# Second layer's output product by one level of Strassen's algorithm instead of a plain product

## The chip, the cores and the metric

The kernel runs on one NeuronCore of one Trainium2 chip. The metric is device time in microseconds (us): of the kernel before, three runs took 610.71, 610.83 and 611.26, median 610.83. Engines are named as in the profile: PE is TensorE (PEld its weight loads), DVE is VectorE, ACT is ScalarE, POOL is GpSimd, SP is SyncE, which issues most DMAs.

## What is computed

A retention layer feeds two dense layers. Its state decays by head, and everything is float32:

```python
for t in range(S):                                   # B, H, S, D = 2, 8, 768, 64
    state = gamma * state + einsum('bhd,bhe->bhde', k[:, :, t], v[:, :, t])
    y[:, :, t] = scale * einsum('bhd,bhde->bhe', q[:, :, t], state)
x = y.transpose(0, 2, 1, 3).reshape(B * S, H * D)    # 1536 x 512
y = ((x @ w_a) * (x @ w_b)) @ w_out                  # 512 -> 1536 -> 512
h = y @ w_in                                         # 512 -> 2048
g = np.maximum(0.01 * h, h)
out = g @ w_out2                                     # 2048 -> 512
```

The inputs of `w_*` reach the device as 64-bit words that are rounded to float32 there.

## The kernel before

Tokens are cut into three tiles of 512 (`t` = 0, 1, 2), features into blocks of 128. A float32 operand is split into a high half, rounded to the matmul's input format (a cast on ACT), and a low half (a subtraction on DVE); `split` (L81) does that, and `mm3` (L88) forms a product from three matmuls: high x high, low x high and high x low. Each matmul loads 128 x 128 weights and streams up to 512 columns into one PSUM bank. PSUM has eight banks.

Four stages follow each other on PE: retention (loop L406), the products with w_a and w_b (`ab_step`), the product with w_out of the first layer (loop L460), and the second layer (loop L505), about 344 us into the span. The order of all instructions is the order of the program text; there is no planner. Weights are loaded by SP into four `raw` buffers, rounded by six operations (`begin_weights`, `round_steps`, on ACT and DVE) and split when `want` asks. `ahead(rate)` rounds weights early, as long as the pool of 80 tiles of 128 x 512 (`slots`) has room. `tnew` gives one of ten further tiles.

In the second layer, for each tile of tokens `t` and each of 16 blocks `f` of inner features, `h2_step` makes one block of h (12 matmuls), ACT scales it by 0.01, DVE takes the maximum, and the result g is split. Two steps later four groups of three matmuls add g (as weights) times the block of w_out into four banks `o`, tokens x 512 outputs:

```python
r = tnew(F32, f"r{t}{f}")
nc.scalar.mul(r, ps, 0.01)
nc.vector.tensor_max(r, r, ps)
g[t, f] = split(r, f"g{t}{f}", tnew)
...
mm3(acc[s], (hi[:, c], lo[:, c]), want("wq", n), n == 0, n == LAST)
```

g lives only until its block has been used. At the end of a tile the four banks are copied and stored. Here `wi` are blocks of w_in, `wq` of w_out. y of tiles 1 and 2 is copied out of PSUM at the end of its stage (`y_out`, L373) and split during the second layer (`y_split`).

Of the kernel before, what the change touches and what calls it, by code (L numbers as in the profile page):

```python
# [63 lines left out]
def retention_moe_kernel(ctx: ExitStack, tc: tile.TileContext, ins, out):  # L64
    nc = tc.nc
    qT, kT, kn, vn, wab, wo, w2, grow, tri, dec = ins

# [20 lines left out]
    def mm3(ps, w, x, first, last):  # L88

        nc.tensor.matmul(ps, w[0], x[0], start=first, stop=False)  # L90
        nc.tensor.matmul(ps, w[0], x[1], start=False, stop=False)  # L91
        nc.tensor.matmul(ps, w[1], x[0], start=False, stop=last)  # L92
# [279 lines left out]

    def y_out(t):  # L373
        for m, ps in enumerate(yps.pop(t)):
            if t == 0:
                y[t, m] = split(ps, f"y{t}{m}")
            else:
                y[t, m] = slots.new(F32, f"yr{t}{m}")
                if m % 2:
                    nc.vector.tensor_copy(y[t, m], ps)  # L380
                else:
                    nc.scalar.copy(y[t, m], ps)
# [91 lines left out]
    g = {}  # L474
    steps = [(t, f) for t in range(NTILE) for f in range(FF2)]
    LAST = FF2 - 1

    def y_split(t, m):
        if t == 1:
            pair = rawp.tile([P, 2, TT], F32R, tag="raw", name=f"y{t}{m}")  # L480
            y[t, m] = split(y[t, m], "", lambda dtype, name: pair[:, int(name == "l"), :])
        else:
            y[t, m] = split(y[t, m], f"y{t}{m}")
        slots.done(1)

    def h2_step(i):
        if i >= len(steps):
            return
        t, f = steps[i]
# [12 lines left out]
    h2_step(0)
    h2_step(1)
    acc = None
    for i, (t, f) in enumerate(steps):  # L505
        if t == 0 and 10 <= f < 10 + KC:
            assert at["round"] == len(order)
            y_split(1, f - 10)
        if t == 1 and 2 <= f < 2 + KC:
            y_split(2, f - 2)  # L510
        if t == 0:
            want("wi", f + 3)
            want("wq", f + 1)
        h2_step(i + 2)
        if f == 0:
            acc = [bank(f"o{t}{s}") for s in range(TT // P)]
        if i == len(steps) - 2:
            continue
        parts = [(f, s) for s in range(TT // P)]
        if i == len(steps) - 1:  # L520
            parts = [(n, s) for s in range(TT // P) for n in (f - 1, f)]
        for n, s in parts:
            c = slice(s * P, (s + 1) * P)
            hi, lo = g[t, n]
            mm3(acc[s], (hi[:, c], lo[:, c]), want("wq", n), n == 0, n == LAST)
            if n < LAST:
                continue
            rows = out[t * TT + s * P:t * TT + (s + 1) * P, :]
            if i == len(steps) - 1 and s == TT // P - 1:
                for copy, dma, tag, d in (  # L530
                    (nc.scalar.copy, nc.scalar, "low", slice(0, TT // 2)),
                    (nc.vector.tensor_copy, nc.sync, "sign", slice(TT // 2, TT)),
                ):
                    o = tmp.tile([P, TT], F32, tag=tag, name=f"end{tag}")
                    copy(o[:, d], acc[s][:, d])
                    dma.dma_start(rows[:, d], o[:, d])
                break
            o = tmp.tile([P, TT], F32, tag=("low", "sign")[s % 2], name=f"o{t}{s}")
            if s % 2:
                nc.vector.tensor_copy(o, acc[s])  # L540
            else:
                nc.scalar.copy(o, acc[s])
            nc.sync.dma_start(rows, o)
        g.pop((t, f))
# [69 lines left out]
```

## Time and profile before

| | |
|---|---|
| median of three runs | 610.83 us |
| the profiled execution | 610.82 us, span 609.0 us |
| PE busy | 600.9 us, 3079 matmuls |
| DVE busy | 363.9 us |
| ACT busy | 216.1 us |
| out stored | 12 pieces, 11 of 256 KB |

The span runs from the first to the last instruction; 1.8 us lie around it. A matmul's record is longer than its distance to the next, since matmuls are pipelined; the distance between two starts is what one costs in a row. The same holds for DVE and ACT, where an operation can start before the one in front has ended.

### The profile page before, as it was taken

How to read it: one execution, taken by the hardware profiler on the slowest of the kernel's cores; microseconds unless marked ns; L12 is line 12 of the kernel's file. 1: busy time of each engine (PE TensorE's matmuls, PEld its weight loads, DVE VectorE, ACT ScalarE, POOL GpSimd, SP SyncE). 2: the span in 40 equal slices, each digit the busy share in tenths (PEclk: the TensorE clock that was granted, in tenths of full speed). 3: DMA queues.
4: the chain of work that ended last, by engine and by line, in shares of the span. 5: the costliest groups of instructions: out<-in, count | busy, mean ns of one | idle time of the engine just before them, and what ended most of it. 6: DMA issues, size and time to landing. Idle time of an engine off the chain costs nothing.

```text
span 609.0 us, 7781 instructions
## 1 busy us (share of the span) xinstructions
PE 600.9 (99%) x3079; PEld 496.8 (82%) x3079; DVE 363.9 (60%) x675; ACT 216.1 (35%) x397; POOL 16.7 (3%) x20
## 2 busy tenths in 40 slices
PE   7999999999999999999999999999999999999997
PEld 4888788888888888888888888888888888888886
DVE  4894767777776867987878688555333222322222
ACT  3672332332233224544334255454322222222221
POOL 4330000000000000000000000000000000000000
PEclk9999999999999999999999999999999999999999
DMA  8991223433333433322433210000100000100001
GB/s 301 382 344 34 97 84 132 138 109 132 112 133 104 138 104 104 108 101 71 136 104 124 84 36 0 1 0 1 69 2 1 0 1 0 70 0 1 0 1 69
DMA packets 19476, 52.22 MB, mean 86 GB/s; under 512 B 2288, under 2 KB 3184, under 8 KB 19440
## 3 DMA queue, kind: packets, MB, share of 16 engines
q1 hardware_dynamic: 19008, 51.32, 24.5%
q8 instruction: 24, 0.39, 0.3%
q10 hardware_dynamic: 432, 0.40, 0.2%
q14 instruction: 12, 0.10, 0.1%
HBM read 48.57 MB, written 3.15 MB: 85 GB/s over the span
## 4 chain that ended last, share of the span: by engine, by line
PE 96%; DVE 1%; DMA 1%; ACT 1%; issue 0%; POOL 0%; SPq 0%; DVEq 0%; POOLq 0%; ACTq 0%
PE o L90 7%; PE h L90 7%; PE h L91 7%; PE o L91 7%; PE o L92 7%; PE h L92 7%; PE y L91 5%; PE y L92 5%; PE y L90 5%; PE pa L92 5%; PE pa L91 5%; PE pa L90 5%; PE pb L92 5%; PE pb L90 5%; PE pb L91 5%; PE sc L240 2%
## 5 line engine op out<-in xcount | busy, mean ns | idle before, releaser
L497 DVE TENSOR_TENSOR r<-r,h 128x512 f32<-128x512 f32 x48 | 33.0, 687 | 117.8 <-ACT r L496 117.8
L496 ACT ACTIVATE r<-h 128x512 f32<-128x512 f32 x48 | 28.7, 598 | 131.5 <-PE h L92 131.5
L339 ACT COPY p<-pa 128x512 f32<-128x512 f32 x36 | 21.0, 587 | 105.6 <-PE pa L92 103.9
L341 DVE TENSOR_TENSOR h<-p,pb 128x512 f32<-128x512 f32 x36 | 24.7, 686 | 46.9 <-PE pb L92 44.7
L246 DVE SCALAR_TENSOR_TENSOR P<-sc,small,causal 128x512 f32<-128x512 f32 x24 | 16.8, 742 | 6.7 <-PE sc L240 6.7
L222 POOL TENSOR_TENSOR qs<-q,cst 128x512 f32<-128x512 f32 x12 | 15.3, 1275 | 22.5 <-DMA q<-in_qT 19.7
L240 PE MATMUL sc<-qs,k 64*128 64x128 f32 x192 | 13.9, 285 | 0.9 <-POOL qs L222 0.9
L240 PEld LDWEIGHTS sc<-qs,k 64*128 64x128 f32 x192 | 11.6, 187 | 3.2 <-POOL qs L222 2.1
L219 ACT ACTIVATE kd<-n,small 128x256 f32<-128x256 f32 x24 | 10.9, 501 | 8.2 <-DMA n<-in_kn 8.0
L298 ACT COPY wk<-cr 64x192 f32<-64x192 f32 (+3 forms) x32 | 10.3, 323 | 6.9 <-DVE cr L281 6.4
L309 PE MATMUL xp<-P,v 128*64 128x128 f32 x192 | 12.6, 274 | 0.0
L324 PE MATMUL xp<-qs,wk 128*128 128x128 f32 x80 | 12.2, 291 | 0.0
L324 PEld LDWEIGHTS xp<-qs,wk 128*128 128x128 f32 x80 | 9.9, 191 | 2.0 <-issue 1.0
L141 DVE SCALAR_TENSOR_TENSOR wi<-wi,sign 128x512 int32<-128x512 int32 x16 | 11.1, 692 | 0.5
L141 DVE SCALAR_TENSOR_TENSOR wq<-wq,sign 128x512 int32<-128x512 int32 x16 | 11.1, 692 | 0.5
L145 DVE CUSTOM_DVE_ANT_0 wq<-wq,low 128x1024 uint16<-128x1024 uint16 x16 | 11.1, 692 | 0.5
L145 DVE CUSTOM_DVE_ANT_0 wi<-wi,low 128x1024 uint16<-128x1024 uint16 x16 | 11.1, 692 | 0.5
L122 ACT ACTIVATE wi<-raw_wi 128x512 f32<-128x512 f32 x16 | 10.7, 670 | 1.9 <-PE pb L91 1.9
L122 ACT ACTIVATE wq<-raw_wq 128x512 f32<-128x512 f32 x16 | 10.7, 671 | 0.1
L309 PEld LDWEIGHTS xp<-P,v 128*64 128x64 f32 x192 | 10.3, 137 | 0.2
L281 DVE SCALAR_TENSOR_TENSOR cr<-cr,small,kv 128x64 f32<-128x64 f32 x32 | 8.9, 279 | 0.9
L145 DVE CUSTOM_DVE_ANT_0 wo<-wo,low 128x1024 uint16<-128x1024 uint16 x12 | 8.3, 693 | 0.4
(3485 smaller groups left out, 1828.4 us busy)
## 6 DMA issues: line engine op xcount, KB each, us to landing
raw_wi<-in_w SPq DMA_DIRECT2D x16, 512.0 KB, 3.2
raw_wq<-in_w SPq DMA_DIRECT2D x16, 512.0 KB, 3.3
raw_a<-in_wab SPq DMA_DIRECT2D x12, 512.0 KB, 3.4
raw_b<-in_wab SPq DMA_DIRECT2D x12, 512.0 KB, 3.3
raw_wo<-in_wo SPq DMA_DIRECT2D x12, 512.0 KB, 3.3
q<-in_qT SPq DMA_DIRECT2D x12, 256.0 KB, 5.3
n<-in_kn SPq DMA_DIRECT2D x12, 256.0 KB, 5.3
v<-in_vn SPq DMA_DIRECT2D x12, 256.0 KB, 5.3
```

The costliest lines, as they stand in the source:

```text
L90: nc.tensor.matmul(ps, w[0], x[0], start=first, stop=False)
L91: nc.tensor.matmul(ps, w[0], x[1], start=False, stop=False)
L92: nc.tensor.matmul(ps, w[1], x[0], start=False, stop=last)
L122: nc.scalar.activation(u, word(raw, F32, 1), AF.Abs)
L141: nc.vector.scalar_tensor_tensor(ui, ui, 3, sign, op0=ALU.logical_shift_left, op1=ALU.bitwise_or)
L145: nc.vector.tensor_tensor(ui, ui, low, op=ALU.add)
L240: nc.tensor.matmul(sc[h][:, c], d["k"][r, c], d["qs"][r, c], start=True, stop=True)
L309: nc.tensor.matmul(xp[r, c], d["v"][:, j * P + h * D:j * P + (h + 1) * D], d["P"][h][:, c], start=j == 0, stop=False,)
L324: nc.tensor.matmul(xp[:, c], d["S"][:, j], d["qs"][:, c], start=False, stop=j == CPT - 1)
L341: nc.vector.tensor_mul(h[t, f], a, pb)
L496: nc.scalar.mul(r, ps, 0.01)
L497: nc.vector.tensor_max(r, r, ps)
```

## The change

The product g @ w_out is done by one level of Strassen's algorithm (Winograd's form, seven products of blocks). The blocks are halves of the inner features (f below and from 8 on), halves of the outputs (256 columns each) and halves of the tokens: tile 0 with the first 256 columns of tile 1, and tile 2 with the last 256. So every operand of a product is a piece of 512 columns and one of 256. Sums of blocks are made in place in the float32 tiles of g and of w_out on DVE; then each operand is split (`prep_form`, one "form" for each product and step j of eight). The order of products is p1, p7, p2, p6, p5, p4, p3; p2 adds onto p1's banks, p3 onto p5's. w_out is now the weight operand and g the moving one, and the output is stored transposed (512 x 1536).

The loop over the second layer runs over f outside and t inside, so that each block of w_in serves all three tiles; all of g is kept. p1 and most of p7 lie inside that loop, a form behind h; the rest follows it, with forms made three ahead (`LEAD`). The last four blocks of w_in are loaded last and rounded only when they are asked for. y is split for all tiles as it leaves PSUM.

```diff
-    order += [(k, f) for f in range(FF2) for k in ("wi", "wq")]
+    late_wi = [("wi", f) for f in range(FF2 - 4, FF2)]
+    order += [(k, f) for f in range(FF2) for k in ("wi", "wq") if (k, f) not in late_wi] + late_wi
...
     def y_out(t):
         for m, ps in enumerate(yps.pop(t)):
-            if t == 0:
-                y[t, m] = split(ps, f"y{t}{m}")
-            else:
...
+            y[t, m] = split(ps, f"y{t}{m}")
...
-        ahead(0.35 if t == 0 else 0.6)
+        ahead(0.35 if t == 0 else 0.6, 9)
...
+    def h2_step(t, f):
         w = want("wi", f)
         ps = bank(f"h2{t}{f}")
...
-        r = tnew(F32, f"r{t}{f}")
-        nc.scalar.mul(r, ps, 0.01)
-        nc.vector.tensor_max(r, r, ps)
-        g[t, f] = split(r, f"g{t}{f}", tnew)
...
+        g[t, f] = g_new(t, f)
+        nc.scalar.mul(g[t, f], ps, 0.01)
+        nc.vector.tensor_max(g[t, f], g[t, f], ps)
...
+    def ablock(i, k, j):
+
+        f = k * HALF + j
+        return g[2 * i, f], g[1, f][:, i * QT:(i + 1) * QT]
...
+    def a_sub(o, p, q):
+        for d, x0, x1 in zip(o, p, q):
+            nc.vector.tensor_sub(d, x0, x1)
+
+    def after_p1(j):
+        a_sub(ablock(0, 0, j), ablock(0, 0, j), ablock(1, 0, j))
+        nc.vector.tensor_sub(bblock(0, 0, j), bblock(0, 1, j), bblock(0, 0, j))
+
+    def before_p7(j):
+        nc.vector.tensor_sub(bblock(0, 1, j), bblock(1, 1, j), bblock(0, 1, j))
+
+    def after_p7(j):
+        a_sub(ablock(0, 0, j), ablock(1, 1, j), ablock(0, 0, j))
+        nc.vector.tensor_sub(bblock(0, 1, j), bblock(1, 1, j), bblock(0, 0, j))
+        for d, x1 in zip(ablock(1, 0, j), ablock(1, 1, j)):
+            nc.vector.tensor_add(d, d, x1)
+
+    def after_p2(j):
+        a_sub(ablock(0, 1, j), ablock(0, 1, j), ablock(0, 0, j))
+        nc.vector.tensor_sub(bblock(1, 0, j), bblock(0, 1, j), bblock(1, 0, j))
...
+    products = {
+        "p1": ((0, 0), (0, 0), None, after_p1),
+        "p7": ((0, 0), (0, 1), before_p7, after_p7),
+        "p2": ((0, 1), (1, 0), None, after_p2),
+        "p6": ((0, 0), (0, 1), None, None),
+        "p5": ((1, 0), (0, 0), None, None),
+        "p4": ((1, 1), (1, 0), None, None),
+        "p3": ((0, 1), (1, 1), None, None),
+    }
+    plan = [(name, j) for name in products for j in range(HALF)]
+    onto = {"p2": "p1", "p3": "p5"}
...
+        w2, x2 = tnew(F32R, f"w{n}"), tnew(F32R, f"x2{n}")
+        hi, lo = new(F32R, f"xh{n}"), new(F32R, f"xl{n}")
+        (a5, a2), b2 = ablock(*a, j), bblock(*b, j)
+        for h, l, src in ((w2[:, 0:QT], w2[:, QT:], b2), (hi, lo, a5), (x2[:, 0:QT], x2[:, QT:], a2)):
+            nc.scalar.copy(h, src)
+            nc.vector.tensor_sub(l, src, as32(h))
...
+        for part in parts:
+            ps = acc[name][part]
+            for m in (range(2) if part == 2 else [part]):
+                w = [w2[:, i * QT + m * P:i * QT + (m + 1) * P] for i in range(2)]
+                if part == 2:
+                    mm3(ps[:, m * QT:(m + 1) * QT], w, x2, first and m == 0, last and m == 1, more)
+                else:
+                    mm3(ps, w, x5, first, last, more)
...
+    for f in range(FF2):
+        for t in range(NTILE):
+            h2_step(t, f)
...
+            if t == 0 and f + 1 < FF2:
+                want("wi", f + 1)
+            if t == 0 and f == FF2 - 1:
+                keep("p1")
+        if f:
+            product(f - 1)
+        prep_form(f)
...
+    for n in range(FF2, FF2 + LEAD - 1):
+        prep_form(n)
...
+    for n in range(FF2 - 1, len(plan) - 2):
+        prep_form(n + LEAD)
+        product(n)
...
+        if name == "p7":
+            keep("p7")
...
+        elif name == "p6":
+            for m, ps in enumerate(acc.pop("p6")):
+                add(u["p1"][m], u["p1"][m], ps)
+                add(u["p7"][m], u["p7"][m], u["p1"][m])
...
+    for m in (2, 0, 1):
+        for n in range(len(plan) - 2, len(plan)):
+            product(n, [m])
+        leave(0, 1, m, u["p1"], add, acc["p3"][m])
```

`keep` copies the three banks of a product to the pool on ACT. `leave` makes a block of the output (a copy on ACT, or a sum on DVE) and stores it from SP.

TensorE's order, one step of the product with w_out. Before (tile 2, f = 2): `o20` to `o23` are the banks of four groups of tokens, the operand behind the arrow is the block of w_out, then g's half.

```order
L90 MATMUL o20_4661<-wq2h_360_3461,g22h_4657 128x512 [waits Activation_49]
L91 MATMUL o20_4661<-wq2l_361_3462,g22h_4657 128x512
L92 MATMUL o20_4661<-wq2h_360_3461,g22l_4658 128x512 [waits DVE_49]
L90 MATMUL o21_4662<-wq2h_360_3461,g22h_4657 128x512
L91 MATMUL o21_4662<-wq2l_361_3462,g22h_4657 128x512
L92 MATMUL o21_4662<-wq2h_360_3461,g22l_4658 128x512 [waits DVE_49]
L90 MATMUL o22_4663<-wq2h_360_3461,g22h_4657 128x512
L91 MATMUL o22_4663<-wq2l_361_3462,g22h_4657 128x512
L92 MATMUL o22_4663<-wq2h_360_3461,g22l_4658 128x512 [waits DVE_49]
L90 MATMUL o23_4664<-wq2h_360_3461,g22h_4657 128x512
L91 MATMUL o23_4664<-wq2l_361_3462,g22h_4657 128x512
L92 MATMUL o23_4664<-wq2h_360_3461,g22l_4658 128x512 [waits DVE_49]
```

Now, form 17 (p2, step 1): `p10` to `p12` are the three banks of p1 that p2 adds to, `xh`/`xl` the halves of the 512 columns, `x2` those of the 256, `w` the weights.

```order
L93 MATMUL p10_3490<-xh17_430_4672,w17_4670 128x512 [waits Activation_49]
L94 MATMUL p10_3490<-xl17_431_4673,w17_4670 128x512 [waits DVE_49]
L95 MATMUL p10_3490<-xh17_430_4672,w17_4670 128x512
L93 MATMUL p11_3491<-xh17_430_4672,w17_4670 128x512
L94 MATMUL p11_3491<-xl17_431_4673,w17_4670 128x512
L95 MATMUL p11_3491<-xh17_430_4672,w17_4670 128x512
L93 MATMUL p12_3492<-x217_4671,w17_4670 128x256 [waits Activation_49]
L94 MATMUL p12_3492<-x217_4671,w17_4670 128x256 [waits DVE_49]
L95 MATMUL p12_3492<-x217_4671,w17_4670 128x256
L93 MATMUL p12_3492<-x217_4671,w17_4670 128x256
L94 MATMUL p12_3492<-x217_4671,w17_4670 128x256
L95 MATMUL p12_3492<-x217_4671,w17_4670 128x256
```

Of twelve matmuls six are now half as wide, and the second and the eighth wait for VectorE.

VectorE's order late in the second layer. Before (tile 2, f = 10 and 11): the maximum that ends g, then the low half of its split.

```order
L497 TENSOR_TENSOR r210_4914<-r210_4914,h2210_4901 128x512 [waits Activation_49]
L85 TENSOR_TENSOR g210l_4918<-r210_4914,g210h_4917 128x512 [waits PE_49,Activation_49]
L497 TENSOR_TENSOR r211_4946<-r211_4946,h2211_4933 128x512 [waits Activation_49]
L85 TENSOR_TENSOR g211l_4950<-r211_4946,g211h_4949 128x512 [waits PE_49,Activation_49]
L497 TENSOR_TENSOR r212_4978<-r212_4978,h2212_4965 128x512 [waits Activation_49]
L85 TENSOR_TENSOR g212l_4982<-r212_4978,g212h_4981 128x512 [waits PE_49,Activation_49]
```

Now, forms 16 and 17 of p2: three low halves (L564), then three sums of blocks (L518, L535).

```order
L564 TENSOR_TENSOR w16_4657<-wq8_326_2952,w16_4657 128x256 [waits Activation_49]
L564 TENSOR_TENSOR xl16_429_4660<-g08_395_3993,xh16_428_4659 128x512 [waits Activation_49]
L564 TENSOR_TENSOR x216_4658<-g18_398_4013,x216_4658 128x256 [waits Activation_49]
L518 TENSOR_TENSOR g08_395_3993<-g08_395_3993,g00_357_3383 128x512 [waits DVE_49]
L518 TENSOR_TENSOR g18_398_4013<-g18_398_4013,g10_358_3399 128x256 [waits DVE_49]
L535 TENSOR_TENSOR wq8_326_2952<-wq0_262_2200,wq8_326_2952 128x256
L564 TENSOR_TENSOR w17_4670<-wq9_328_3022,w17_4670 128x256 [waits Activation_49]
L564 TENSOR_TENSOR xl17_431_4673<-g09_400_4073,xh17_430_4672 128x512 [waits Activation_49]
L564 TENSOR_TENSOR x217_4671<-g19_403_4093,x217_4671 128x256 [waits Activation_49]
L518 TENSOR_TENSOR g09_400_4073<-g09_400_4073,g01_360_3451 128x512 [waits DVE_49]
L518 TENSOR_TENSOR g19_403_4093<-g19_403_4093,g11_363_3471 128x256 [waits DVE_49]
L535 TENSOR_TENSOR wq9_328_3022<-wq1_266_2252,wq9_328_3022 128x256
```

Two operations a block have become six a form, with the low halves of form 17 behind the sums of form 16.

## Rows read from the trace of the kernel before

**Rows 1.** The page's part 1, and two lines of its 40 slices.

```profile
PE 600.9 (99%) x3079; PEld 496.8 (82%) x3079; DVE 363.9 (60%) x675; ACT 216.1 (35%) x397; POOL 16.7 (3%) x20
...
DVE  4894767777776867987878688555333222322222
...
PEclk9999999999999999999999999999999999999999
```

**Rows 2.** Longest waits: who waited for whom, total, times, longest.

```profile
ACT r L496 <- PE h L92: 131.5, 47, 3.5
DVE r L497 <- ACT r L496: 117.8, 42, 3.4
```

**Rows 3.** Stretches: length, busy PE, PEld, DVE, ACT, POOL, clock, DMA, GB/s.

```profile
246.20:343.90 97.70, 97.70 (x433) 80.90 (x432) 79.68 (x150) 40.04 (x70) 0.00 (x0) 1.00 0.31 103
343.90:605.50 261.60, 261.59 (x1155) 216.26 (x1153) 105.19 (x167) 83.54 (x144) 0.00 (x0) 1.00 0.04 15
```

**Rows 4.** Timeline (start, length, engine): matmuls of h and o in a row.

```profile
589.69 0.39 PE L90 MATMUL h<-y21h,wi14h 128*128 128x512 f32 x1
...
595.13 0.39 PE L90 MATMUL h<-y21h,wi15h 128*128 128x512 f32 x1
```

**Rows 5.** Timeline where the products of the first layer begin.

```profile
48.63 0.97 PEld L324 LDWEIGHTS xp<-qs,wk 128*128 128x128 f32 x8 [0.17 <-ACT wk L298]
...
49.51 0.19 PEld L90 LDWEIGHTS pa<-x0h,a0h 128*128 128x128 f32 x1
...
49.62 0.19 PEld L91 LDWEIGHTS pa<-x0l,a0h 128*128 128x128 f32 x1
...
49.85 0.39 PE L91 MATMUL pa<-x0l,a0h 128*128 128x512 f32 x1
49.86 0.19 PEld L92 LDWEIGHTS pa<-x0h,a0l 128*128 128x128 f32 x1
```

**Rows 6.** Groups by line and form: busy us, mean ns of one, idle before.

```profile
L497 DVE TENSOR_TENSOR r<-r,h 128x512 f32<-128x512 f32 x48 | 33.0, 687 | 117.8 <-ACT r L496 117.8
...
L281 DVE SCALAR_TENSOR_TENSOR cr<-cr,small,kv 128x64 f32<-128x64 f32 x32 | 8.9, 279 | 0.9
...
L540 DVE COPY o<-o 128x512 f32<-128x512 f32 x5 | 3.3, 684 | 2.7 <-PE o L92 2.7
...
L279 DVE COPY cr<-kv 128x64 f32<-128x64 f32 x8 | 1.7, 216 | 0.8 <-PE kv L269 0.8
...
L496 ACT ACTIVATE r<-h 128x512 f32<-128x512 f32 x48 | 28.7, 598 | 131.5 <-PE h L92 131.5
...
L298 ACT COPY wk<-cr 64x256 f32<-64x256 f32 x8 | 3.2, 404 | 2.9 <-DVE cr L281 2.8
```

**Rows 7.** Timeline of DVE: subtractions in a row; rounding between its ends.

```profile
287.74 0.42 DVE L137 TENSOR_SCALAR sign<-raw_wi 128x512 int32<-128x512 int32 x1
...
290.20 0.68 DVE L85 TENSOR_TENSOR hs17l<-h,hs17h 128x512 fp32r<-128x512 f32 x1
...
415.03 0.68 DVE L85 TENSOR_TENSOR y<-yr,y 128x512 fp32r<-128x512 f32 x1
415.63 0.68 DVE L85 TENSOR_TENSOR wi15l<-wi,wi15h 128x512 fp32r<-128x512 f32 x1
```

**Rows 8.** Timeline of the last copies.

```profile
605.57 0.37 ACT L535 COPY endlow<-o 128x256 f32<-128x256 f32 x1 [0.82 <-PE o L92]
...
605.98 0.42 DVE L535 COPY endsign<-o 128x256 f32<-128x256 f32 x1 [2.48 <-ACT endlow L535]
```

**Rows 9.** DMA issues: size, median us from issue to landing.

```profile
out<-o SPq DMA_DIRECT2D x11, 256.0 KB, 2.1
...
out<-endsign SPq DMA_DIRECT2D x1, 128.0 KB, 1.7
```

More of the change, by code (lines that the diff above doesn't have):

```diff
@@ L30 @@
 KC = DM // P
-NSLOT = 80
+NSLOT = 81
 NRAW = 4
@@ L36 @@
 COUNT = {"a": FF1, "b": FF1, "wo": FF1, "wi": FF2, "wq": FF2}
+HALF = FF2 // 2
+QT = DM // 2
+LEAD = 3
 TOP = float(np.array((255 << 20) - 1, np.int32).view(np.float32))
@@ L86, in split, with mm3 @@
         return hi, lo
[L88 to L92, printed above, removed]
+    def mm3(ps, w, x, first, last, more=False):
+        nc.tensor.matmul(ps, w[0], x[0], start=first, stop=False, skip_group_check=more)
+        nc.tensor.matmul(ps, w[0], x[1], start=False, stop=False, skip_group_check=more)
+        nc.tensor.matmul(ps, w[1], x[0], start=False, stop=last, skip_group_check=more)
     weights = {}
@@ L165, in ahead @@
         while at["due"] >= 1 and at["round"] < at["load"] and slots.room() >= 1 + reserve:
+            if order[at["round"]] in late_wi:
+                return
             round_weights()
             at["due"] -= 1
-            if at["begin"] < at["load"]:
+            if at["begin"] < at["load"] and order[at["begin"]] not in late_wi:
                 begin_weights()
@@ L374, in y_out @@
         for m, ps in enumerate(yps.pop(t)):
-            if t == 0:
-                y[t, m] = split(ps, f"y{t}{m}")
-            else:
[L378 to L382, printed above, removed]
+            y[t, m] = split(ps, f"y{t}{m}")
     attention_constants()
@@ L465, in retention_moe_kernel @@
         if t == NTILE - 1 and f >= FF1 - 4:
-            want(*(("wi", 0), ("wi", 1), ("wi", 2), ("wq", 0))[f - FF1 + 4])
+            if f >= FF1 - 2:
+                want("wi", f - FF1 + 2)
         y_mm(t, f)
@@ L470, in retention_moe_kernel, with g_new @@
         slots.tick()
-        ahead(0.35 if t == 0 else 0.6)
[L474 to L489, printed above, removed]
+        ahead(0.35 if t == 0 else 0.6, 9)
+    g, wq, u = {}, {}, {}
+    def g_new(t, f):
+        if f < FF2 - 4:
+            return slots.new(F32, f"g{t}{f}")
+        if t != 1:
+            if t == 0:
+                g["raw", f] = rawp.tile([P, 2, TT], F32, tag="raw", name=f"g{f}")
+            return g["raw", f][:, t // 2, :]
+        if f < FF2 - 2:
+            return tnew(F32, f"g{t}{f}")
+        return tmp.tile([P, TT], F32, tag="low", name=f"g{t}{f}")
+    def h2_step(t, f):
         w = want("wi", f)
@@ L494, in h2_step @@
             mm3(ps, (w[0][:, c], w[1][:, c]), y[t, kc], kc == 0, kc == KC - 1)
-        r = tnew(F32, f"r{t}{f}")
-        nc.scalar.mul(r, ps, 0.01)
-        nc.vector.tensor_max(r, r, ps)
-        g[t, f] = split(r, f"g{t}{f}", tnew)
-        if f == LAST and t == 0:
-            slots.done(2 * KC)
[L502 to L517, printed above, removed]
-            continue
[L519 to L544, printed above, removed]
@@ new lines, in h2_step, with bblock @@
+        g[t, f] = g_new(t, f)
+        nc.scalar.mul(g[t, f], ps, 0.01)
+        nc.vector.tensor_max(g[t, f], g[t, f], ps)
+        if t == NTILE - 1:
+            slots.done(2)
+        if f == FF2 - 1:
+            slots.done(2 * KC)
+    def ablock(i, k, j):
+        f = k * HALF + j
+        return g[2 * i, f], g[1, f][:, i * QT:(i + 1) * QT]
+    def bblock(k, o, j):
+        f = k * HALF + j
+        if f not in wq:
+            while ("wq", f) not in rounded:
+                round_weights()
+            wq[f] = rounded.pop(("wq", f))
+        return wq[f][:, o * QT:(o + 1) * QT]
@@ new lines, in retention_moe_kernel, with prep_form @@
+    plan = [(name, j) for name in products for j in range(HALF)]
+    onto = {"p2": "p1", "p3": "p5"}
+    forms, acc = {}, {}
+    def prep_form(n):
+        if n >= len(plan):
+            return
+        name, j = plan[n]
+        a, b, before, after = products[name]
+        if before:
+            before(j)
+        new = tnew if n < FF2 else slots.new
+        w2, x2 = tnew(F32R, f"w{n}"), tnew(F32R, f"x2{n}")
[4 more added lines that the diff above has]
+            nc.vector.tensor_sub(l, src, as32(h))
+        forms[n] = (hi, lo), (x2[:, 0:QT], x2[:, QT:]), w2
+        if after:
+            after(j)
@@ new lines, in product @@
+    def product(n, parts=range(3)):
+        name, j = plan[n]
+        if j == 0 and 0 in parts:
+            acc[name] = acc[onto[name]] if name in onto else [bank(f"{name}{m}") for m in range(3)]
+        x5, x2, w2 = forms[n]
+        first = j == 0 and name not in onto
+        last = j == HALF - 1
+        more = name in onto
+        for part in parts:
[6 more added lines that the diff above has]
+                    mm3(ps, w, x5, first, last, more)
+        if n >= FF2 and 2 in parts:
+            slots.done(2)
@@ new lines, in keep, with store @@
+    def keep(name):
+        u[name] = []
+        for m, ps in enumerate(acc.pop(name) if name != "p1" else acc[name]):
+            u[name].append(slots.new(F32, f"u{name}{m}"))
+            nc.scalar.copy(u[name][m], ps)
+    def store(i, o, m, c):
+        rows = slice(o * QT, o * QT + P), slice(o * QT + P, (o + 1) * QT)
+        if m < 2:
+            nc.sync.dma_start(out[rows[m], 2 * i * TT:(2 * i + 1) * TT], c)
+        else:
+            for k in range(2):
+                at0 = TT + i * QT
+                nc.sync.dma_start(out[rows[k], at0:at0 + QT], c[:, k * QT:(k + 1) * QT])
@@ new lines, in leave @@
+    def leave(i, o, m, with_, op, ps):
+        c = slots.new(F32, f"c{i}{o}{m}")
+        if with_ is None:
+            nc.scalar.copy(c, ps)
+        else:
+            op(c, with_[m], ps)
+        store(i, o, m, c)
+        slots.done(1)
+    for f in range(FF2):
+        for t in range(NTILE):
+            h2_step(t, f)
+            slots.tick()
+            if t == 0 and f + 1 < FF2:
[5 more added lines that the diff above has]
+        prep_form(f)
+        slots.tick()
+        if f < FF2 - 4:
+            ahead(1.4, 4)
@@ new lines, in retention_moe_kernel @@
+    for n in range(FF2, FF2 + LEAD - 1):
+        prep_form(n)
+    add, sub = nc.vector.tensor_add, nc.vector.tensor_sub
+    for n in range(FF2 - 1, len(plan) - 2):
+        prep_form(n + LEAD)
+        product(n)
+        slots.tick()
+        name, j = plan[n]
+        if j < HALF - 1:
+            continue
+        if name == "p7":
+            keep("p7")
+        elif name == "p2":
+            for m, ps in enumerate(acc.pop("p2")):
+                leave(0, 0, m, None, None, ps)
+        elif name == "p6":
+            for m, ps in enumerate(acc.pop("p6")):
+                add(u["p1"][m], u["p1"][m], ps)
+                add(u["p7"][m], u["p7"][m], u["p1"][m])
+        elif name == "p5":
+            for m, ps in enumerate(acc["p5"]):
+                leave(1, 1, m, u["p7"], add, ps)
+        elif name == "p4":
+            for m, ps in enumerate(acc.pop("p4")):
+                leave(1, 0, m, u["p7"], sub, ps)
@@ L608 @@
     ]
-    out = nc.dram_tensor("out", (NT, DM), F32, kind="ExternalOutput").ap()
+    out = nc.dram_tensor("out", (DM, NT), F32, kind="ExternalOutput").ap()
     with _tile.TileContext(nc) as tc:
@@ L612 @@
     r = _run(nc, [arrays], core_ids=[0])
-    return r.results[0]["out"]
+    return np.ascontiguousarray(r.results[0]["out"].T)
```

1 line of the change is left out of this document (removed).

## The prediction

> **What bounds the kernel now.** [...] The waits then say who waits for whom: ScalarE and VectorE each stand for over 100 us before the pair of operations that makes g, behind TensorE [rows 2]. The stretches settle it: in the second layer (343.9 to 605.5) TensorE is busy for 261.59 of 261.60 us, VectorE for 105.19, ScalarE for 83.54 [rows 3]. Only matmul time counts there, until another engine needs longer than TensorE in some part of it.
>
> A matmul of 512 columns costs its distance to the next: 24 of them from 589.69 to 595.13, so 0.2267 us [rows 4]. The product with w_in is 48 blocks of 12 matmuls, that with w_out 48 of 12 as well: 576 x 0.2267 = 130.6 us each, 261.2 together, which is the stretch. The change leaves the first 130.6 and rebuilds the second.
>
> **TensorE's part.** Seven products of eight steps make 56 forms. A form has 6 matmuls of 512 columns and 6 of 256 (the halved middle tile of tokens), so 336 of each replace 576. No matmul of this kind with 256 columns is in the trace. From below: a load of 128 weight columns can follow the one before it after 0.11 us (49.51 to 49.62; and eight in 0.97 us of which the last lasts 0.19, so (0.97 - 0.19) / 7 = 0.111 [rows 5]), and half of 0.2267 is 0.113; so 0.111. From above: half the columns gain nothing, 0.227. [...] I take 0.116, between 0.111 and 0.120, because the load is seen at 0.11 and begins as the matmul in front of it does (49.85 and 49.86 [rows 5]). Then 336 x 0.2267 + 336 x 0.116 = 76.2 + 39.0 = 115.2: 15.4 us less than 130.6.
>
> [...]
>
> **VectorE's part.** Removed in the second layer: 48 splits of g, 16 of w_out. Added: for every form three subtractions (256, 512, 256 columns) that make the low halves, and for the first three products sums of blocks, in place. ScalarE makes the high halves with casts of 256, 512 and 256 columns; a copy of 256 is 404 ns and one of 512 about 600 [rows 6], so 1.4 us against TensorE's form of 6 x 0.2267 + 6 x 0.116 = 2.06: not the bound.
>
> Subtractions of 512 columns that don't hang on each other follow at 0.60 us though each lasts 0.69 [rows 7]. For 256 there is no row: from below half of it, 0.30, from above 0.60. Operations on 64 and 512 columns last 279 and 687 ns with two inputs, 216 and 684 ns as copies [rows 6], so a column is 0.911 or 1.045 ns, and 256 columns fewer leave 0.37 or 0.33. I take 0.35, between these. [...]
>
> A form in the third product (p2) is 0.35 + 0.60 + 0.35, then three sums of 0.60 + 0.35 + 0.35: 2.60 us, against 2.06 on TensorE, which so waits 0.54 a form. From the fourth product on there are no sums, 1.30 a form, and VectorE gets ahead again. The subtractions are queued behind the sums of the form before, and TensorE's second matmul of a form waits for one of them: that is the path.
>
> Ahead of p2: when the last block of w_in ends, one form (2.06) is still queued on TensorE. ScalarE scales (0.60), VectorE takes the maximum (0.60 to the next start) and subtracts blocks of w_out (0.46 until it can be used), ScalarE casts (0.40), VectorE makes two low halves (0.35 + 0.69), with 0.1 of signals: 3.2, less 0.23 for the matmul that needs no low half, less 2.06: a wait of about 1.0. Then five sums (0.60 + 0.35 + 0.35 + 0.60 + 0.35 = 2.25) come in front of form 16: its low half is there 0.60 + 0.35 + 2.25 + 0.35 = 3.55 us after that of form 15, where TensorE needs 2.06: 1.5. With 8 x 0.54 = 4.3 (seven steps inside p2, one into p6) the waits are 6.8 us. With 0.30 for 256 columns they are 1.0 + 1.2 + 8 x 0.34 = 4.9, with 0.60 they are 1.3 + 2.7 + 8 x 1.54 = 16.3.
>
> Steps 11 to 14 of w_in: the last four of its blocks are rounded there, no longer ahead. VectorE per step: three maxima 1.80, five operations of rounding 2.46 (287.74 to 290.20 [rows 7]), a cast that it waits for 0.77, that block's low half 0.60, the block of w_out with its cast 0.92, the form 1.30, five sums 2.25: 10.1. TensorE: 36 x 0.2267 + 2.06 = 10.22. No slack is left. Two products hold three accumulators each, which leaves two banks for h: a block waits for the maximum of the block two before it. Alone that comes 1.4 us after its end (0.60 + 0.69 [rows 6] and signals), under the 2.72 of the block between; behind a rounding it is late. Bounds 0 and 4 x 0.8 = 3; I take 1.0. Steps 0 to 10 need at most 7 us of VectorE and are covered; so are 8 more subtractions for y, less 4 copies, in the stretch before, where VectorE has 79.68 busy of 97.70 us [rows 3].
>
> Ends of products: three copies on ScalarE after p7 and after p2, six sums on VectorE after p6 (about 4 us, while three forms, 6.2 us, are ready), three each after p5 and p4. LEAD 3 covers them; without that lead they cost up to 4 us. Stores rise from 12 to 16, all but the last covered by matmuls. The tail: before, copies of 0.37 and 0.42 us one after the other and 1.7 to land [rows 8, 9]; now one sum of 0.69 and a store of 256 KB, which lands in 2.1: 0.2 more.
>
> **Sum.** -15.4 + 6.8 + 1.0 + 0.2 = -7.4. The profiled execution took 610.82 (span 609.0 and 1.8 around it) and the median is 610.83, so nothing is corrected: 603.4 us.
>
> **Rivals.**
> One: VectorE is the bound for longer, and the kernel is slower. Every subtraction waits for a ScalarE cast; if they then don't overlap, an operation costs its whole length, 0.69 and (by the line) 0.455. A form in p2 is then 3.2, which is 1.14 too long and 9.1 over eight; the two waits ahead are 1.1 and 2.3; steps 11 to 14 take 11.5 against 10.22, so 5.2. Sum -15.4 + 12.5 + 5.2 + 0.2 = +2.5: 613.3. It decides from a p2 form of about 3.0 on. For it: a split of g in the trace does wait for its cast each time. Against it: where casts run ahead, as in [rows 7], they overlap, and ScalarE has the time to run ahead in p2.
>
> Two: a matmul of 256 columns is no cheaper than one of 512; load and columns one after the other would be 0.111 + 0.113 = 0.224. With 672 x 0.2267 = 152.3 the work grows by 21.8; a form takes 2.72, over VectorE's 2.60, and of the waits about 1.1 stays: 634. It decides from 0.143 on (15.4 - 336 x 0.027 = 6.3 of gain against waits that have shrunk to 5.2 + 0.9 + 0.2). Against it: 0.11 between loads, beside running matmuls. [...]
>
> Three: the waits stay small. With 0.111 for the short matmul (-17.1), 0.30 for the short subtraction (5.3 of waits) and no loss in steps 11 to 14 it is 599.2. With VectorE never late it is 593.9, but that wants a p2 form of 2.06, and six operations even at 0.60 and 0.30 are 2.40.
>
> Four: it doesn't do what it says, because waits of 14 to 16 us, from parts of rival one, give all of the saving back: 609.6 to 612.
>
> **Chances.** The forecast's case (600.5 to 607.5) 0.62; three 0.11; one and four (607.5 to 615) 0.16; two 0.10; else 0.01. I count 0.2%, 1.2 us, as what a measurement of this kernel can tell from no change. Faster by more: 0.62 + 0.11 + 0.03 from the lower end of one and four = 0.76; within it 0.06; slower 0.18. Range 598.5 to 611.5: outside are two, the upper part of one, and sums that are wholly hidden, about 0.18.
>
> **What would show it.** In the profile after: matmuls of 512 columns 0.227 apart and of 256 columns 0.111 to 0.120; TensorE without waits up to the 11th step; its waits in one place, from the end of w_in to the first forms of p6, near 6.8 us in all, with VectorE busy without a gap there; then none until the end. Wrong it is if the short matmuls stand above 0.14 apart, if a wait shows at each block of h from step 9 on, or if p6, p5 and p4 wait as well.

## The result

The changed kernel takes 604.43 us (median of four runs, 604.18 to 605.06), the kernel before in the same session 611.05 (610.71 to 611.39): a ratio of 0.9893, with a 95% interval of 0.9876 to 0.991. Forecast were 603.4 us in 598.5 to 611.5. The profiled execution took 604.18 us, its span is 602.4; against the profiled execution of before (610.82 and 609.0) that is 6.6 us less, where 7.4 less had been forecast.

The page of the kernel after, part 1 and the slices that answer to [rows 1]:

```profile
PE 590.7 (98%) x3175; PEld 492.0 (82%) x3175; DVE 439.9 (73%) x880; ACT 244.3 (41%) x499; POOL 16.9 (3%) x20
...
PE   7999999999999999999999999999999998999997
...
DVE  4894767877777777996979565454567887998773
...
PEclk9999999999999999999999999999999999999999
```

One of TensorE's slices in the last quarter, the 34th, is now at 8, and in the two behind it VectorE, which had fallen to 2 or 3 there, is at 9. The granted clock stays at full (1.00 in each stretch below). The stretches say the same in microseconds (length, then busy time of TensorE, of the weight loads, of VectorE, ScalarE and GpSimd, granted clock, DMA share, GB/s), against [rows 3]:

```profile
343.50:425.00 81.50, 81.50 (x380) 68.22 (x380) 46.26 (x90) 28.59 (x58) 0.00 (x0) 1.00 0.04 14
425.00:465.00 40.00, 40.00 (x190) 33.54 (x188) 25.96 (x52) 13.67 (x27) 0.00 (x0) 1.00 0.00 1
465.00:505.90 40.90, 40.90 (x193) 34.27 (x192) 32.59 (x66) 16.32 (x34) 0.00 (x0) 1.00 0.00 1
505.90:531.50 25.60, 22.18 (x113) 16.87 (x111) 25.12 (x59) 17.36 (x42) 0.00 (x0) 1.00 0.02 6
531.50:600.00 68.50, 67.13 (x383) 58.60 (x383) 51.95 (x109) 35.68 (x88) 0.00 (x0) 1.00 0.12 41
```

Up to 505.9 TensorE has no gap. From there to 531.5, which is the last form of p7 and the whole third product (p2), VectorE is busy for 25.12 of 25.60 us and TensorE for 22.18: here the two have changed places. (VectorE's missing 0.48 us lie ahead of 506.81, where it waits for ScalarE's casts; behind that it has no gap.) After it TensorE is the bound again (its 1.37 us without work at the end are the tail). The list of TensorE's waits (engine, tile and line; engine, tile and line waited for; total us, times, longest) holds nothing else in the second layer:

```profile
PE p L94 <- DVE xl L564: 2.8, 10, 1.1
...
PE p L93 <- ACT xh L563: 0.6, 1, 0.6
```

These 3.4 us are less than what was lost, because a busy matmul lasts longer (0.39 us for 512 columns) than its distance to the next (0.23). By starts the waits are 6.4 us, as the timeline of TensorE (start, length, line, operation, tile, and in brackets the idle time before it) shows:

```profile
505.92 0.28 PE L95 MATMUL p<-x,w 128*128 128x256 f32 x1
...
506.83 0.49 PE L93 MATMUL p<-xh,w 128*128 128x512 f32 x1 [0.63 <-ACT xh L563]
...
507.55 0.50 PE L94 MATMUL p<-xl,w 128*128 128x512 f32 x1 [0.23 <-DVE xl L564]
...
507.89 0.40 PE L95 MATMUL p<-xh,w 128*128 128x512 f32 x1
...
509.53 0.39 PE L93 MATMUL p<-xh,w 128*128 128x512 f32 x1
...
511.04 0.50 PE L94 MATMUL p<-xl,w 128*128 128x512 f32 x1 [1.11 <-DVE xl L564]
511.37 0.39 PE L95 MATMUL p<-xh,w 128*128 128x512 f32 x1
...
513.58 0.50 PE L94 MATMUL p<-xl,w 128*128 128x512 f32 x1 [0.18 <-DVE xl L564]
...
516.13 0.50 PE L94 MATMUL p<-xl,w 128*128 128x512 f32 x1 [0.18 <-DVE xl L564]
...
531.41 0.50 PE L94 MATMUL p<-xl,w 128*128 128x512 f32 x1 [0.18 <-DVE xl L564]
```

From 505.92 to 506.83 are 0.91 us where 0.12 would do, so 0.79 are lost; in the same way 0.50 before 507.55, and 1.28 between 509.53 and 511.04 (1.51 less 0.23). Then comes one wait a form, eight times, 2.545 us apart: the timeline's idle time says 0.18, by starts it is 0.345. Behind each such wait the next matmul follows 0.34 us later and not 0.23 (511.04 to 511.37), which is 0.11 more. Together: 0.79 + 0.50 + 0.11, then 1.28 + 0.11, then 8 x 0.455, that is 1.4 + 1.4 + 3.6 = 6.4.

What VectorE does in those 2.545 us, to be read against [rows 7]:

```profile
512.51 0.41 DVE L564 TENSOR_TENSOR w<-wq,w 128x256 fp32r<-128x256 f32 x1
512.84 0.68 DVE L564 TENSOR_TENSOR xl<-g,xh 128x512 fp32r<-128x512 f32 x1
513.45 0.41 DVE L564 TENSOR_TENSOR x<-g,x 128x256 fp32r<-128x256 f32 x1
513.78 1.02 DVE L518 TENSOR_TENSOR g<-g,g 128x512 f32<-128x512 f32 x2
514.72 0.41 DVE L535 TENSOR_TENSOR wq<-wq,wq 128x256 f32<-128x256 f32 x1
515.05 0.41 DVE L564 TENSOR_TENSOR w<-wq,w 128x256 fp32r<-128x256 f32 x1
515.39 0.68 DVE L564 TENSOR_TENSOR xl<-g,xh 128x512 fp32r<-128x512 f32 x1
```

Three low halves (L564), three sums (L518 for g, L535 for w_out), and the next form at once, with no idle time at any row. An operation of 512 columns stands 0.60 us before the next, one of 256 columns 0.335; (2 x 0.60 + 4 x 0.335) = 2.54. TensorE's L94 matmul at 513.58 starts when the low half begun at 512.84 has ended (513.52): the sums of one form delay the low half of the next.

TensorE without waits, one form of p2, answers to [rows 4 and 5]:

```profile
515.08 0.28 PE L95 MATMUL p<-x,w 128*128 128x256 f32 x1
515.20 0.28 PE L93 MATMUL p<-x,w 128*128 128x256 f32 x1
515.20 0.19 PEld L94 LDWEIGHTS p<-x,w 128*128 128x128 f32 x1
515.32 0.28 PE L94 MATMUL p<-x,w 128*128 128x256 f32 x1
515.32 0.19 PEld L95 LDWEIGHTS p<-x,w 128*128 128x128 f32 x1
...
515.44 0.28 PE L95 MATMUL p<-x,w 128*128 128x256 f32 x1
515.44 0.19 PEld L93 LDWEIGHTS p<-xh,w 128*128 128x128 f32 x1
515.56 0.39 PE L93 MATMUL p<-xh,w 128*128 128x512 f32 x1
```

A matmul of 256 columns costs 0.12 us to the next. Its weights are loaded beside the matmul in front, as for 512 columns (a matmul starts at 504.87, the load of the next one at 504.88): each load in these rows begins within 0.01 us of that matmul's start. Load and columns one after the other, the 0.224 of the second rival, are not what this run shows.

The tail, against [rows 8]:

```profile
598.25 0.39 PE L95 MATMUL p<-xh,w 128*128 128x512 f32 x1
598.67 0.69 DVE L609 TENSOR_TENSOR c<-up,p 128x512 f32<-128x512 f32 x1 [0.67 <-PE p L95]
```

The last matmul starts at 598.25 and the span ends 4.14 us later; before, the last one started at 605.10 and the span ended 3.92 later.

### The profile page after: what moved, and what is told of

Its sections match the earlier page's. It is cut to its first block, busy times and chain, and to the rows that moved or that the text cites. A ratio compares the mean times of both kernels' runs of the same rounds, so it can differ in the third digit from the quotient of the medians.

```text
span 602.4 us, 8333 instructions
## 1 busy us (share of the span) xinstructions
PE 590.7 (98%) x3175; PEld 492.0 (82%) x3175; DVE 439.9 (73%) x880; ACT 244.3 (41%) x499; POOL 16.9 (3%) x20
## 3 DMA queue, kind: packets, MB, share of 16 engines
HBM read 48.57 MB, written 3.15 MB: 86 GB/s over the span
## 4 chain that ended last, share of the span: by engine, by line
PE 92%; DVE 6%; ACT 1%; DMA 1%; issue 0%; POOL 0%; SPq 0%; DVEq 0%; POOLq 0%
PE h L93 7%; PE h L94 7%; PE h L95 7%; PE y L94 5%; PE y L93 5%; PE y L95 5%; PE p L94 5%; PE p L95 5%; PE p L93 5%; PE pa L94 5%; PE pa L95 5%; PE pa L93 5%; PE pb L95 5%; PE pb L93 5%; PE pb L94 5%; PE sc L246 2%
## 5 line engine op out<-in xcount | busy, mean ns | idle before, releaser
L497 DVE TENSOR_TENSOR g<-g,h 128x512 f32<-128x512 f32 x48 | 32.5, 684 | 49.8 <-ACT g L496 49.8
L496 ACT ACTIVATE g<-h 128x512 f32<-128x512 f32 x48 | 28.4, 597 | 81.4 <-PE h L95 81.3
L94 PE MATMUL p<-xl,w 128*128 128x512 f32 x112 | 45.1, 403 | 2.8 <-DVE xl L564 2.8
L93 PE MATMUL p<-xh,w 128*128 128x512 f32 x112 | 44.1, 394 | 0.6 <-ACT xh L563 0.6
L95 PE MATMUL p<-xh,w 128*128 128x512 f32 x112 | 43.6, 389 | 0.0
L564 DVE TENSOR_TENSOR xl<-g,xh 128x512 fp32r<-128x512 f32 x56 | 38.5, 688 | 2.3
L563 ACT CAST w<-wq 128x256 fp32r<-128x256 f32 x56 | 22.7, 405 | 39.9 <-PE p L95 30.3
L563 ACT CAST xh<-g 128x512 fp32r<-128x512 f32 x56 | 34.6, 617 | 0.0
L564 DVE TENSOR_TENSOR w<-wq,w 128x256 fp32r<-128x256 f32 x56 | 23.6, 421 | 11.5 <-ACT w L563 11.5
L95 PE MATMUL p<-x,w 128*128 128x256 f32 x112 | 31.7, 283 | 0.0
L94 PE MATMUL p<-x,w 128*128 128x256 f32 x112 | 31.7, 283 | 0.0
L93 PE MATMUL p<-x,w 128*128 128x256 f32 x112 | 31.4, 281 | 0.0
L94 PEld LDWEIGHTS p<-xl,w 128*128 128x128 f32 x112 | 21.1, 189 | 8.9 <-DVE xl L564 5.9
L95 PEld LDWEIGHTS p<-xh,w 128*128 128x128 f32 x112 | 21.1, 188 | 4.3
L93 PEld LDWEIGHTS p<-xh,w 128*128 128x128 f32 x112 | 21.2, 189 | 3.9 <-ACT xh L563 0.8
L564 DVE TENSOR_TENSOR x<-g,x 128x256 fp32r<-128x256 f32 x56 | 23.4, 418 | 0.0
L93 PEld LDWEIGHTS p<-x,w 128*128 128x128 f32 x112 | 21.3, 190 | 2.3
L94 PEld LDWEIGHTS p<-x,w 128*128 128x128 f32 x112 | 21.3, 190 | 2.1
L518 DVE TENSOR_TENSOR g<-g,g 128x512 f32<-128x512 f32 (+1 forms) x40 | 21.8, 577 | 0.0
```

Of the source, the lines that this page charges most:

```text
L93: nc.tensor.matmul(ps, w[0], x[0], start=first, stop=False, skip_group_check=more)
L94: nc.tensor.matmul(ps, w[0], x[1], start=False, stop=False, skip_group_check=more)
L95: nc.tensor.matmul(ps, w[1], x[0], start=False, stop=last, skip_group_check=more)
L496: nc.scalar.mul(g[t, f], ps, 0.01)
L497: nc.vector.tensor_max(g[t, f], g[t, f], ps)
L518: nc.vector.tensor_sub(d, x0, x1)
```

## The experiments

Two theories were set against each other. A: VectorE's queue sets the pace of p2, because the sums of a form stand ahead of the next form's low halves, and it is the length of that queue that counts. B: the forms are made too few ahead, or wait for free tiles, so that the number of operations matters little and the lead matters. The times below stand against 604.43; the kernel before was run again beside each group, at 610.77 and 611.33, and the ratios, with 95% intervals, are to that.

**No sums in p2.** The three subtractions after each form of p2 are left out, so p4 and p3 work on other numbers; all matmuls stay.

```diff
-        "p2": ((0, 1), (1, 0), None, after_p2),
+        "p2": ((0, 1), (1, 0), None, None),
```

> Leaves out the sums of blocks that follow each form of p2 (so p4 and p3 use blocks that were never changed). Theory A: TensorE waits in p2 because VectorE's queue holds three sums (1.27 us) between the low halves of two forms, 2.55 us a form against 2.09. Without them a form is 1.27: the eight waits of 0.45 us go, the two waits ahead (1.4 and 1.4) stay, 604.4 - 3.6 = 600.8. Theory B: tiles are short (the casts of a form wait until TensorE has used the form four before), and VectorE's sums only fill time that would be idle: 604.4, unchanged.

Measured: 601.28 us (601.11 to 601.94), ratio 0.9845 (0.983 to 0.9859). TensorE's waits are down to those at the opening, two for form 15 and one for form 16 (about 1.4 us each form by starts):

```profile
507.34 0.50 PE L93 MATMUL p<-xh,w 128*128 128x512 f32 x1 [0.64 <-ACT xh L563]
508.07 0.50 PE L94 MATMUL p<-xl,w 128*128 128x512 f32 x1 [0.23 <-DVE xl L564]
511.55 0.50 PE L94 MATMUL p<-xl,w 128*128 128x512 f32 x1 [1.11 <-DVE xl L564]
```

The eight regular waits are gone, 3.6 us by starts, and the median is 3.15 lower. That is theory A, and 2.8 us of waits are left that the sums of p2 have nothing to do with.

**One operation more in p2.** VectorE gets one more pass over 256 columns in each form of p2, the maximum of a block of w_out with itself, which changes no value.

```diff
     def after_p2(j):
         ...
+        nc.vector.tensor_max(bblock(0, 0, j), bblock(0, 0, j), bblock(0, 0, j))
```

> One more operation of 256 columns on VectorE after each form of p2 (a maximum of a block with itself, which changes nothing). Theory A: each costs TensorE its 0.335 us, eight of them 2.7: 607.1. Theory B: they fall into idle time, 604.4.

Measured: 607.55 us (606.73 to 607.67), ratio 0.9946 (0.9929 to 0.9962), so 3.1 us more for eight operations. On TensorE the waits are now 2.88 us apart, where they were 2.545:

```profile
513.80 0.49 PE L94 MATMUL p<-xl,w 128*128 128x512 f32 x1 [0.49 <-DVE xl L565]
516.68 0.50 PE L94 MATMUL p<-xl,w 128*128 128x512 f32 x1 [0.52 <-DVE xl L565]
519.56 0.50 PE L94 MATMUL p<-xl,w 128*128 128x512 f32 x1 [0.51 <-DVE xl L565]
```

Each form has become longer by just the distance of one short VectorE operation, 0.335 us: what is added to VectorE there is on the path one to one. In the other direction only 0.455 of the 1.27 us of a form's sums come back, since TensorE's own 2.09 us are then the longer.

**A lead of four forms.** The rival's own remedy.

```diff
-LEAD = 3
+LEAD = 4
```

> Forms are made four ahead instead of three, with the same tiles. Theory A: VectorE's rate sets p2, so a longer lead gains nothing, 604.4. Theory B (forms come too late in the order of the program, or tiles are short): up to 3.6 us less, 600.8, or more time if the casts then wait longer for tiles.

Measured: 604.94 us (604.12 to 605.8), ratio 0.9899 (0.9883 to 0.9915), the same ten waits for VectorE and the same 6.4 us. Taken alone this says little about the lead, since `LEAD` moves a form only against the copies and sums at the ends of products: VectorE's operations stand in the same order through the whole of p2 in both traces. What it moves there, ScalarE's casts of form 19, come 1.4 us earlier and gain nothing.

Against the other half of theory B, the free tiles, the trace of the changed kernel speaks by itself. From form 21 on, ScalarE's casts do wait about 1.3 us a form for TensorE to free a tile, but in all of p2 a cast is done 2.4 to 6.6 us before VectorE takes it up. For form 21, the cast and the subtraction that uses it:

```profile
515.76 0.41 ACT L563 CAST w<-wq 128x256 fp32r<-128x256 f32 x1 [1.32 <-PE p L95]
```

```profile
522.69 0.42 DVE L564 TENSOR_TENSOR w<-wq,w 128x256 fp32r<-128x256 f32 x1
```

With the two runs above, theory B falls: neither tiles nor this lead hold p2 up. That forms made earlier on VectorE itself would not help does not follow, and the run after the next shows that they do.

**p2 and p6 in turn.** Same instructions, but the forms of p2 (with sums) alternate with those of p6 (without).

```diff
-    for n in range(FF2 - 1, len(plan) - 2):
-        prep_form(n + LEAD)
+    seq = [15] + [n for j in range(HALF) for n in (2 * HALF + j, 3 * HALF + j)] + list(range(4 * HALF, len(plan)))
+    made = 1
+    for s, n in enumerate(seq[:-2]):
+        while made < min(s + LEAD + 1, len(seq)):
+            prep_form(seq[made])
+            made += 1
```

> Nothing left out: after p7 the forms of p2 and p6 alternate (p2 step 0, p6 step 0, p2 step 1, ...) instead of eight of p2 and then eight of p6. Theory A: a pair costs VectorE 2.55 + 1.27 = 3.8 us and TensorE 2 x 2.09 = 4.2, so the eight waits in p2 go and the two ahead of it (2.8 us) stay: 604.4 - 3.6 = 600.8. Theory B: the number of tiles in flight is the same, so the waits stay, 604.4.

Measured: 601.96 us (601.64 to 602.49), ratio 0.9855 (0.984 to 0.9869). Two forms then cost VectorE 2.54 + 1.27 = 3.81 us and TensorE 2 x 2.09 = 4.18, and the regular waits end after one of 0.33 + 0.11; 3.2 us are left in all. The work that made p2 late isn't too much, it stands too close together. The median lies 1.2 us above what had been expected; 0.44 of that is the one regular wait that is left, and for the rest see the table below.

**Two forms made earlier.** Forms 16 and 17, the first two of p2, are made inside the last step of the product with w_in, and TensorE takes them ahead of form 15, the last of p7.

```diff
+            if t < 2 and f == FF2 - 1:
+                prep_form(FF2 + t)
+                slots.tick()
 ...
-    for n in range(FF2, FF2 + LEAD - 1):
-        prep_form(n)
 ...
+    seq = [16, 17, 15] + list(range(18, len(plan)))
```

> Nothing left out: the first two forms of p2 are made inside the last step of w_in, behind the maxima of tiles 0 and 1, and TensorE takes them before the last form of p7. Theory A: the two waits ahead of p2 (1.4 + 1.4) are there because at the end of w_in only one form is queued, while VectorE still has a maximum, a form and five sums to do; with two forms more in the queue (4.2 us) they go, the other six waits of p2 stay: 604.4 - 2.8 - 2 x 0.45 = 600.7, or 601.6 if VectorE's queue is only shifted. If the end of w_in were limited by TensorE's own switch between products, nothing changes, 604.4.

Measured: 602.18 us (601.71 to 603.42), ratio 0.9857 (0.9842 to 0.9872). The opening costs 0.89 instead of 2.8 us, and six of the regular waits follow (6 x 0.455 = 2.7), 3.6 in all and so 2.8 less. The median fell by 2.25, less than the 2.8 that had been expected at the least (see the table below).

**Both.** The two edits together; the forms are taken as 16, 17, 15, 24, 18, 25, 19 and so on.

```diff
+    seq = [16, 17, 15, 24, 18, 25, 19, 26, 20, 27, 21, 28, 22, 29, 23, 30] + list(range(31, len(plan)))
```

> Nothing left out: both the early forms and the alternation of p2 and p6. Theory A: all waits of TensorE in the second layer go, 604.4 - 6.4 = 598.0. If the two share a cause, or VectorE is late anyway, it is 600 to 601.

Measured: 599.52 us (599.06 to 600.09), ratio 0.9811 (0.9796 to 0.9825). This is the fastest version, 4.9 us under the changed kernel and 11.8 under the kernel before beside it; the waits do not all go, as theory A had it, and 598.0 is missed. One wait is left, 0.89 by starts, and the stretch that had 22.18 us of TensorE now has 24.98:

```profile
514.68 0.50 PE L94 MATMUL p<-xl,w 128*128 128x512 f32 x1 [0.61 <-DVE xl L564]
```

```profile
505.90:531.50 25.60, 24.98 (x144) 21.70 (x143) 24.98 (x60) 16.14 (x40) 0.00 (x0) 1.00 0.00 1
```

**Eight plain products.** The same halves and the same order of work, but eight products of blocks without sums in place of the seven: 64 forms.

```diff
-        "p1": ((0, 0), (0, 0), None, after_p1),
-        ...
-        "p3": ((0, 1), (1, 1), None, None),
+        f"q{i}{o}{k}": ((i, k), (k, o), None, None)
+        for i, o in ((0, 0), (0, 1), (1, 1), (1, 0)) for k in range(2)
```

> The same loops, layout and forms without Strassen: the eight plain products of the same blocks (64 forms instead of 56) and no sums of blocks. If the saving is the eight forms that Strassen drops, less VectorE's waits: TensorE 64 x 2.09 = 133.8 for the product with w_out instead of 117.0 (16.7 more), waits of about 0.9 at the last block of w_in instead of 6.4, 604.4 + 16.7 - 5.5 = 615.6, slower than the kernel before by some 4.6, which is what halves of 256 columns and the new order cost. If instead the new order of loops had brought the gain, it would stay near 604.

Measured: 615.46 us (615.02 to 615.72), ratio 1.0074 (1.0059 to 1.0089). With TensorE free of waits but for 0.3 us, this is what the cut into halves and the new order of work cost together: 4.7 us, of which 2.1 are the dearer matmuls of 256 columns, 384 x (0.1188 - 0.1133). Strassen's step then takes 11.0 off it: eight forms of 2.09 us are 16.7 less, and 6.1 of waits come back, which is 10.6; the profiled executions give 10.8 from the first to the last matmul of the second layer (265.02 against 254.24).

**Two operations more in steps 11 to 14.** Two extra passes over 512 columns in each of these steps, of values that they don't change, right behind the maximum of the middle tile. This tests the claim of no slack, which the profile after could not show, since no wait stands there.

```diff
+        if t == 1 and 11 <= f < 15:
+            for _ in range(2):
+                nc.vector.tensor_max(g[t, f], g[t, f], g[t, f])
```

> Two more operations of 512 columns on VectorE (maxima of a block with itself, which change nothing) in each of the steps 11 to 14 of w_in, where the prediction said that VectorE has no slack (10.1 of 10.2 us a step). If that is so, 4 x 2 x 0.60 = 4.8 us are added, less the 0.1 a step that is left: 608.8. If VectorE's waits in these steps (for casts and for TensorE) hold slack, since the profile after shows no wait of TensorE there, it stays at 604.4.

Measured: 610.07 us (609.68 to 611.11), ratio 0.9983 (0.9974 to 0.9993): 5.6 us more. Four new waits appear, each of a block of h for the maximum two blocks before it:

```profile
PE h L93 <- DVE g L497: 4.1, 4, 1.4
```

By starts they come to 5.2 together with the 0.11 behind each, for eight operations of about 0.7 us (0.684 is the length of 512 columns in the trace after). So under 1 us of slack was there in the four steps: forecast right as to the room, and the cost of 1.0 that was laid on it didn't come, because VectorE just kept pace.

**What the waits account for.** The starts of the first and the last matmul of the second layer in each profiled execution, what lies between them, and the waits by starts in that stretch, all in us:

| kernel | first | last | between | against after | waits | against after |
|---|---|---|---|---|---|---|
| after | 344.00 | 598.25 | 254.24 | | 6.42 | |
| no sums in p2 | 344.51 | 595.19 | 250.68 | -3.56 | 2.79 | -3.63 |
| one operation more | 343.88 | 600.80 | 256.93 | +2.69 | 9.09 | +2.67 |
| lead 4 | 345.63 | 599.87 | 254.24 | 0.00 | 6.41 | -0.01 |
| p2 and p6 in turn | 344.87 | 595.99 | 251.12 | -3.12 | 3.24 | -3.18 |
| two forms earlier | 344.59 | 596.02 | 251.43 | -2.81 | 3.60 | -2.82 |
| both | 345.34 | 594.13 | 248.79 | -5.45 | 0.89 | -5.53 |
| two operations more | 345.62 | 605.20 | 259.58 | +5.34 | 11.60 | +5.18 |

Within 0.2 us the waits are all that moves the second layer. Where it begins scatters from 343.9 to 345.6 by what lies ahead of it, which is the same code in all eight. The medians, set against 604.43, all lie 0.45 to 0.71 us above what the waits give, the one with a lead of four forms too, which has the same waits as the changed kernel. Against its 604.94 the other six follow the waits within 0.2 us. So the 604.43 of four runs in another session is a reference some 0.5 us low for this comparison; why is not shown.

## Why the prediction was right

The sum by its terms, forecast and measured:

- TensorE's matmuls: -15.4, measured -13.1. From the start of the first matmul of the second layer to that of the last were 260.89 us (344.21 to 605.10), now 254.24; without the waits of 6.42 they are 247.82, so 13.1 less. This is the term that was mis-sized. A short matmul was put at 0.116 between 0.111 and 0.120; it is 0.119 on the mean, 39.9 us for 336 where 39.0 had been reckoned (1.0). And the long ones, put at 0.2267 as in [rows 4], are 0.230 on the mean in forms that hold short ones, up to 0.236 (all long ones: 207.9 us where 911 distances of 0.2267 are 206.5, so 1.4), which no row of before could show. For the short one 0.120, the upper of the two values it was taken between, was the nearer. No row of before shows that 0.120, and no run the 0.116 taken under it: both were the author's estimate, and in their place the run after shows 0.119 on the mean and 0.120 on the median.
- The waits at the end of w_in and in p2: 6.8, measured 6.4, in the place named and from the cause named: the eight regular ones by the experiments without sums and with one more operation, those at the opening by the two forms made earlier, which took 1.9 of their 2.8. In parts: the opening 1.0 (its working adds up to 0.91), measured 1.4; form 16 1.5, measured 1.4; then 8 x 0.54, measured 8 x 0.455, since VectorE's form is 2.545 and not 2.60 (a short operation 0.335, not 0.35) and TensorE's 2.09 and not 2.06.
- Steps 11 to 14: 1.0, measured 0. The room was as small as forecast, but its lower bound held.
- The tail: 0.2, measured 0.2 (4.14 against 3.92 us).
- The second layer also begins 0.2 us earlier (344.00 against 344.21), which no term had, and which is within what it scatters by (the table above).

In two decimals, -13.07 + 6.42 + 0 + 0.22 - 0.21 = -6.64, as measured. The errors were on both sides, +2.3 from the matmuls, -1.4 from waits that stayed smaller, and the forecast's nearness owes something to that.

Of the rivals, one (VectorE the bound for longer) needed a p2 form of 3.0 us and got 2.545, since casts ran ahead (by 2.4 us and more) and the subtractions overlapped. Two needed 0.143 for the short matmul. Three needed short matmuls at 0.111 and short subtractions at 0.30, and both came out higher. Four needed 14 us of waits. What the forecast did expect of the later products, that behind the first form of p6 they wait for nothing, is in the list of waits; no wait there is for a DMA, whose share from 465 to 531.5 is at most 0.02.

What made the opening dearer than the forecast had it can be read off the trace:

```profile
503.96 0.39 PE L93 MATMUL p<-xh,w 128*128 128x512 f32 x1
...
504.80 0.69 DVE L497 TENSOR_TENSOR g<-g,h 128x512 f32<-128x512 f32 x1 [2.03 <-ACT g L496]
...
505.40 0.42 DVE L525 TENSOR_TENSOR wq<-wq,wq 128x256 f32<-128x256 f32 x1
...
505.85 0.41 ACT L563 CAST w<-wq 128x256 fp32r<-128x256 f32 x1 [1.09 <-DVE wq L525]
...
506.16 0.61 ACT L563 CAST xh<-g 128x512 fp32r<-128x512 f32 x1
506.29 0.42 DVE L564 TENSOR_TENSOR w<-wq,w 128x256 fp32r<-128x256 f32 x1 [0.47 <-ACT w L563]
...
506.81 0.69 DVE L564 TENSOR_TENSOR xl<-g,xh 128x512 fp32r<-128x512 f32 x1
```

The product with w_in is done at 503.96, where form 14, the one still queued, begins; form 15's second matmul starts at 507.55. These 3.59 us had been put at 3.2. The subtraction for xl starts 0.52 us behind the one for w and not 0.35, since it needs ScalarE's cast of xh, which ends at 506.77: 0.17. The other 0.22 lie where one engine hands over to the next, 0.32 in all where 0.1 had been put. The matmul behind, 0.11 late, had no term. With the 0.91 of the working that makes 1.41. TensorE's first matmul of form 15 waits for xh as well, until 506.83, but this costs nothing more, because the second one waits for the low half, as forecast. No run moved that cast alone.

## What to carry over

Work taken from the bound engine lands on another, and what counts is not that engine's share over a stage but its queue between the moments at which the first has a stock: here VectorE was busy for 182 of the second layer's 256 us, and the bound in 25 of them. Reckon per form, on both engines, by the distances between starts and not by the length of one operation, and look at what stands in the queue ahead of the operand that the bound engine takes next. A larger `LEAD`, which left VectorE's order in p2 as it was, bought nothing (604.94); another order of the same instructions on VectorE bought 4.9 us (599.52).

## What the runs showed of the hardware

- Matmuls of 256 columns of this kind stand 0.120 us apart on the median (0.113 at the least), against 0.2267 for 512; the first in a row after a long one is followed after 0.114 on the median, the later ones after 0.120. The long ones in a form with short ones take 0.230 on the mean and up to 0.236.
- A matmul that had to wait for VectorE delays the one behind it too, by 0.11 us, in all ten cases; a wait counted by starts (0.455) is more than twice the idle time that the profile gives for it (0.18).
- VectorE's operations of 256 columns with two inputs last 0.417 and stand 0.335 apart, those of 512 last 0.684 and stand 0.60 apart, so each overlaps the next by about 0.08 us.
- The granted clock stayed at full through all these waits, the longest 1.28 us (1.00 in the stretch from 505.9 to 531.5).
